# Weights requested ahead of batch 1's rows, O of group 0 directly behind its H, and batch 1 on the later batches' path, in a fused attention and MoE kernel

## Chip, cores and metric

One core of one Trainium2 chip. The metric is device time in microseconds (us) of one execution. Most executions of a kernel here agree within 1 to 2%. A few executions are in a slower state (those over 1.5% above the fastest of their kernel count as slow): every ratio uses fast runs alone, the medians are over all runs, and every profiled run was a fast one. Times inside an execution are counted from the start of the profiled span, which is some 2 us shorter than the device time.

## The reference, cut to what matters

```python
# q, k, v: (8 batches, 8 heads, 576 positions, 64), f32
rel    = pos[:, None] - pos[None, :]
scores = q @ k.T / 8 - slope[h] * abs(rel)
scores = where((rel >= 0) & (rel < 128), scores, -1e9)   # a causal window of 128
x      = softmax(scores) @ v                             # laid out as (4608 tokens, 512)
h      = x @ w_in                                        # w_in  512 x 2048
g      = h * sigmoid(beta * h)
out    = g @ w_out                                       # w_out 2048 x 512
```

The kernel works in bf16. It makes the columns of x batch by batch (attention) and eats them in nine groups of 512 tokens: **H** of a group is 16 x 4 matmuls with W1 (w_in), **O** is 4 x 4 *quarters* of four matmuls each with W2 (w_out). A batch has 576 tokens, so group 0 needs only batch 0, group 1 needs batch 1 too.

## The kernel before: the parts that matter

Every q, k and v row block is requested by SyncE as f32, cast to bf16 by GpSimd and, from batch 2 on, transposed by a DMA that SyncE issues as well. Weights are requested by GpSimd and cast on the way.

```python
def get(what, b, sb):                 # 128 rows of one of q, k, v: SyncE
    f = fst_pool.tile([P, H, D], F32, ...)                       # 13 buffers
    return nc.sync.dma_start(out=f[0:rows], in_=src[b, :, ...].rearrange("h p d -> p h d"))

def cast_qk(b, sb):                   # GpSimd, 4 buffers
    ...
    nc.gpsimd.tensor_copy(out=t[0:rows, 0], in_=fs.pop(("q", b, sb))[0:rows])
    return nc.gpsimd.tensor_copy(out=t[0:rows, 1], in_=fs.pop(("k", b, sb))[0:rows])

def DT(b, sb):                        # the transpose by DMA: SyncE
    nc.sync.dma_start(out=QK[b % 2][...], in_=src[0:rows]..., transpose=True)

def load_w2(n):                       # a quarter of W2: GpSimd; load_w1 is alike
    return nc.gpsimd.dma_start(out=W2[:, bass.ts(n, 4), :], in_=W2v[:, bass.ts(n, 4), :])

def SC(b, m, p):                      # later path: scores of two heads into SS (one tile)
    ...  # TensorE matmuls from QK, exp on ScalarE into pt, mask on VectorE
```

Batches 0 and 1 have a path of their own ("pairs"): rows come as pairs of heads, TensorE transposes them (`TP`), the bias is added by a matmul with a table (`SP_`), and the last 64 rows of each of these batches are done separately (the *tail*: `TT`, `SCT`, `PV`, `X`). The order of the opening before:

```python
# batch 0's pairs ... first W1 requests in between ...
after(get_pair(1, 0), w1[1])           # batch 1's rows behind two quarters of W1
... # the other rows of batch 1, the tails of batches 0 and 1
cast_pair(1, 0); cast_pair(1, 1); cast_v(1, 0); cast_v(1, 1); cast_pair(1, 2)
w2 = [load_w2(0), load_w2(1)]          # W2 behind most casts of batch 1
cast_pair(1, 3)
w2 += [load_w2(2), load_w2(3)]
... # TensorE: H of group 0, batch 1's pairs and tail 0 between; then H of group 1 with
    # tail 1 and the 16 + 8 O quarters of groups 0 and 1 between; then groups 2 to 8
```

The softmax here doesn't subtract the row's maximum and nothing guards it: scores larger than these inputs give would overflow.

## Time and profile before

| | before |
|---|---|
| device time, median of 4 runs | 352.47 us (349.71 to 357.34) |
| profiled span, mean granted clock | 350.1 us, 0.989 |
| TensorE busy, matmuls | 324.5 us (93%), 2289 |
| SyncE's DMA queue | 145,312 packets, 38.30 MB |
| GpSimd's DMA queue | 6,944 packets, 13.11 MB |
| first H / H of group 1 / group 2 | 23.0 / 61.70 / 109.3 us |

Of these 4 runs the one of 357.34 us is slow by that rule. The other three have a median of 351.21 us, and the later jobs measured this kernel at 350.86 to 351.08.

The prediction shows the slices, the stretches and the timelines of TensorE and ScalarE. One view of the kernel before is to be added, since the argument turned on it: SyncE's requests (columns: start, us that the issue took, queue, line, operation, tile and source, how many). These are batch 1's rows, requested after most of W1 had come and before any of W2 was asked for:

```profile
27.47 2.57 SPq L242 DMA_DIRECT2D fst<-in_q_dram  x1
...
31.80 1.91 SPq L234 DMA_DIRECT2D fst<-in_k_dram  x2
33.80 0.46 SPq L242 DMA_DIRECT2D fst<-in_q_dram  x1
```

Most requests of this stretch take 0.5 to 1.3 us each to issue; with W2 in flight, from 43 us on, three of four take 3.3 to 6.2.

### The profile page before, as it was taken

How to read it: one execution, taken by the hardware profiler on the slowest of the kernel's cores; microseconds unless marked ns; L12 is line 12 of the kernel's file. 1: busy time of each engine (PE TensorE's matmuls, PEld its weight loads, DVE VectorE, ACT ScalarE, POOL GpSimd, SP SyncE). 2: the span in 40 equal slices, each digit the busy share in tenths (PEclk: the TensorE clock that was granted, in tenths of full speed). 3: DMA queues.
4: the chain of work that ended last, by engine and by line, in shares of the span. 5: the costliest groups of instructions: out<-in, count | busy, mean ns of one | idle time of the engine just before them, and what ended most of it. 6: DMA issues, size and time to landing. Idle time of an engine off the chain costs nothing.

```text
span 350.1 us, 6218 instructions
## 1 busy us (share of the span) xinstructions
PE 324.5 (93%) x2289; PEld 151.4 (43%) x2289; DVE 192.3 (55%) x422; ACT 206.9 (59%) x396; POOL 111.5 (32%) x208
## 2 busy tenths in 40 slices
PE   6886886998999999998999999999999999999995
PEld 2442443443444444443444444444444444544442
DVE  7445576454754776476627763674477455614500
ACT  2545663548856776566657775675687566426511
POOL 4793624633735333503131324242200100010010
PEclk9899999899999999999999999999999999999999
DMA  7998999999999999991286989799311201120012
GB/s 176 228 195 204 194 186 202 177 201 220 217 230 237 239 211 226 212 198 48 57 182 133 182 175 227 129 222 166 93 32 53 77 30 47 30 99 0 30 62 90
DMA packets 152285, 51.79 MB, mean 148 GB/s; under 512 B 143664, under 2 KB 149824, under 8 KB 152256
## 3 DMA queue, kind: packets, MB, share of 16 engines
q1 hardware_dynamic: 145312, 38.30, 57.5%
q0 software_dynamic: 6944, 13.11, 14.9%
q8 instruction: 18, 0.29, 0.4%
q14 instruction: 11, 0.09, 0.1%
HBM read 36.71 MB, written 9.44 MB: 132 GB/s over the span
## 4 chain that ended last, share of the span: by engine, by line
PE 67%; ACT 11%; DVE 10%; DMA 6%; issue 3%; SPq 3%; POOL 0%; POOLq 0%; ACTq 0%
PE ops L530 31%; PE hps L507 26%; ACT pt L434 8%; DVE gT L515 4%; DVE pt L438 4%; PE SS L424 3%; DMA W<-in_moe_w_in_dram 3%; ACT sig L514 2%; SPq L234 2%; DMA fst<-in_k_dram 2%; PE pv L463 2%; PE pv L459 1%; DMA fst<-in_q_dram 1%; DVE xn L349 1%; PE SS L324 1%
## 5 line engine op out<-in xcount | busy, mean ns | idle before, releaser
L507 PE MATMUL hps<-XT,W 128*128 128x512 bf16 x560 | 141.5, 382 | 5.6 <-DVE gT L515 4.0
L530 PE MATMUL ops<-W,gT 128*128 128x512 bf16 x576 | 139.0, 379 | 0.0
L515 DVE SCALAR_TENSOR_TENSOR gT<-sig,hps 128x512 bf16<-128x512 bf16 x140 | 94.7, 683 | 76.4 <-ACT sig L514 75.7
L514 ACT ACTIVATE sig<-hps,beta_h 128x512 bf16<-128x512 f32 x140 | 95.8, 694 | 61.4 <-PE hps L507 56.1
L434 ACT ACTIVATE pt<-SS,bias 128x256 bf16<-128x256 f32 (+1 forms) x192 | 75.0, 478 | 11.4 <-PE SS L424 11.3
L507 PEld LDWEIGHTS <-W 128*128 128x128 bf16 x576 | 51.5, 98 | 62.6 <-issue 11.8
L530 PEld LDWEIGHTS <-gT 128*128 128x128 bf16 x576 | 52.4, 98 | 58.1 <-issue 2.1
L543 POOL DMA_DIRECT2D out_dram<-osb x34 | 18.4, 542 | 136.2 <-ACT osb L536 134.4
L438 DVE TENSOR_TENSOR pt<-pt,mask 128x1024 bf16<-128x1024 bf16 x48 | 38.0, 792 | 26.7 <-ACT pt L434 26.7
L536 ACT ACTIVATE osb<-ops 128x512 f32<-128x512 f32 x36 | 21.6, 600 | 44.6 <-PE ops L530 44.6
L265 POOL CAST vs<-fst 128x512 bf16<-128x512 f32 (+1 forms) x40 | 25.0, 636 | 37.4 <-DMA fst<-in_v_dram 32.5
L252 POOL CAST bst<-fst 128x512 bf16<-128x512 f32 (+1 forms) x32 | 20.7, 647 | 32.5 <-DMA fst<-in_q_dram 22.9
L349 DVE TENSOR_TENSOR xn<-pv,zs 128x256 bf16<-128x256 f32 (+1 forms) x64 | 26.9, 421 | 1.7
L348 DVE RECIPROCAL zs<-pv 128x4 f32<-128x4 f32 (+1 forms) x80 | 14.0, 176 | 22.3 <-PE pv L463 13.3
L253 POOL CAST bst<-fst 128x512 bf16<-128x512 f32 (+1 forms) x32 | 21.0, 656 | 10.2 <-DMA fst<-in_k_dram 10.0
L463 PE MATMUL pv<-vs,pt 128*128 128x65 bf16 x240 | 21.4, 193 | 0.0
L424 PE MATMUL SS<-qkT 64*128 64x256 bf16 (+2 forms) x240 | 18.9, 252 | 2.6 <-ACT pt L434 2.4
L463 PEld LDWEIGHTS <-pt 128*128 128x128 bf16 x240 | 16.5, 97 | 8.4
L341 ACT ACTIVATE pt<-SS 128x768 bf16<-128x768 f32 (+1 forms) x12 | 10.6, 881 | 15.5 <-PE SS L335 15.4
L424 PEld LDWEIGHTS <-qkT 64*128 64x128 bf16 x240 | 8.4, 94 | 23.1 <-issue 22.7
L459 PE MATMUL pv<-vs,pt 128*128 128x65 bf16 x192 | 17.9, 193 | 0.0
L459 PEld LDWEIGHTS <-pt 128*128 128x128 bf16 x192 | 15.2, 98 | 5.6
(78 smaller groups left out, 148.5 us busy)
## 6 DMA issues: line engine op xcount, KB each, us to landing
out_dram<-osb POOLq DMA_DIRECT2D x34, 256.0 KB, 3.3
fst<-in_q_dram SPq DMA_DIRECT2D x32, 256.0 KB, 4.8
fst<-in_v_dram SPq DMA_DIRECT2D x32, 256.0 KB, 4.0
fst<-in_k_dram SPq DMA_DIRECT2D x24, 256.0 KB, 5.2
fst<-in_k_dram SPq DMA_DIRECT2D x24, 128.0 KB, 4.0
W<-in_moe_w_in_dram POOLq DMA_DIRECT2D x4, 512.0 KB, 9.5
W<-in_moe_w_out_dram POOLq DMA_DIRECT2D x4, 512.0 KB, 11.1
fst<-in_q_dram SPq DMA_DIRECT2D x8, 128.0 KB, 3.3
```

The source lines that it names most:

```text
L265: return nc.gpsimd.tensor_copy(out=VS[b % 2][0:rows, sb, :, 0:D], in_=fs.pop(("v", b, sb))[0:rows])
L349: nc.vector.tensor_tensor(out=xn, in0=pv[0:nq, :, 0:D], in1=zs[0:nq].broadcast_to([nq, 4, D]), op=ALU.mult)
L424: nc.tensor.matmul(o, lhsT=qk[64 * e : 64 * e + 64, 1, p, P * kb : P * kb + P], rhs=qk[64 * e : 64 * e + 64, 0, p, P * kb : P * kb + nq], ...
L434: nc.scalar.activation(out=pt[:, e, cols], in_=sps[:, e, cols], func=ACTF.Exp, scale=qscale, bias=bias[:, half, h : h + 1],)
L438: nc.vector.tensor_tensor(out=pt[:], in0=pt[:], in1=masks[m][:], op=ALU.mult)
L459: nc.tensor.matmul(pv[:, hl, 0 : D + 1], lhsT=weights(b, qb - 1, h, 1), rhs=vs[:, qb - 1, h, 0 : D + 1], start=True, stop=False,)
L463: nc.tensor.matmul(pv[:, hl, 0 : D + 1], lhsT=weights(b, qb, h, 0), rhs=vs[:, qb, h, 0 : D + 1], start=qb == 0, stop=True,)
L507: nc.tensor.matmul(hps[:], lhsT=W1[:, c, bass.ts(j, P)], rhs=XT[:, c, c0 : c0 + TOKG], start=(c == 0), stop=(c == NDM - 1),)
L514: nc.scalar.activation(out=sig[:], in_=hps[:], func=ACTF.Tanh, scale=beta_h[:, j : j + 1])
L515: nc.vector.scalar_tensor_tensor(out=gts[g][:, j, :], in0=sig[:], scalar=1.0, in1=hps[:], op0=ALU.add, op1=ALU.mult)
L530: nc.tensor.matmul(ops_, lhsT=gT[:, j, i * P : i * P + P], rhs=W2[:, j, :], start=(j == 0), stop=(j == NFF - 1),)
L536: nc.scalar.mul(osb[:], ops_, 0.5)
```

## The change

Its intent: let TensorE go from H of group 0 straight to its O, by asking for all weights at once; drop batch 1's pair path, which costs TensorE transposes, table matmuls and permuting matmuls; and start batch 0 a little sooner by borrowing PSUM banks. The diff, cut to its core:

```diff
+    def room(b, wide, shape, name):          # new: batch 0 may use H's PSUM banks
+        if b == 0 and wide:
+            return psum_h.tile(shape, F32, name=name + "h", tag="hps")
+        return psum_t.tile(shape, F32, name=name, tag="t")
 ...
-    for b in range(2, B):                    # the later path
+    for b in range(1, B):
 ...
+            cast_pair(0, 3)
             w1.append(load_w1(0))
-            cast_pair(0, 3)
-            w1.append(load_w1(1))
+            cast_v(0, 2)
+            cast_v(0, 3)
+            w1 += [load_w1(n) for n in range(1, 4)]
+            betas()
 ...
-            betas()
+            w2 = [load_w2(0)]
             constants_late()
+            w2 += [load_w2(n) for n in range(1, 4)]
+            constants_masks()
 ...
-        after(get_pair(1, 0), w1[1])         # and all of the pair path of batch 1
+        b1 = blocks(1, [tail])               # rows, casts, DMA transposes of batch 1
+        b1.insert(6, tail_casts)             # casts of batch 0's tail: behind block 0's
+        gate = True
+        for job in b1:
+            r = job()
+            if gate:
+                after(r[0], w1[0])
+                gate = False
 ...
+        att[4:4] = tails                     # batch 0's tail behind four score groups
 ...
+        items = HG(0)[3:] + two(0) + OG(0, 2) + OG(0, 3)
+        spread(items, len(items) - 5, len(items) - 1, NP)
```

More of the change, by code (lines that the diff above doesn't have):

```diff
@@ L130, in constants @@
         make_identity(nc, ident[:])
+        make_identity(nc, identf[:])
         nc.gpsimd.iota(
@@ L188, in betas @@
         bps = psum_t.tile([P, NFF], F32, name="bps", tag="t")
-        make_identity(nc, identf[:])
         nc.tensor.transpose(out=bps[:], in_=bflat[:], identity=identf[:])
@@ L216 @@
     staged = {}
+    moved = set()
     def get(what, b, sb):
@@ L263, in cast_v @@
     def cast_v(b, sb):
+        moved.add(("v", b, sb))
         rows = ROWS[sb]
@@ L342, in SP_ @@
         pts[b, vis, p] = pt
+    WIDE = (("B", 0), ("B", 1))
+    def room(b, wide, shape, name):
+        if b == 0 and wide:
+            return psum_h.tile(shape, F32, name=name + "h", tag="hps")
+        return psum_t.tile(shape, F32, name=name, tag="t")
     PLACES = {0: ((0, 0),), 1: ((0, 128), (1, 256)), 2: ((1, 128), (2, 0)), 3: ((2, 384), (3, 256))}
@@ L357, in PVP @@
         pt = pts.pop((b, vis, p))
-        pv = psum_t.tile([P, 4, 66], F32, name="pv", tag="t")
+        pv = room(b, (vis, p) in WIDE, [P, 4, 66], "pv")
         q0 = 0 if vis == "A" else 2
@@ L372, in XP @@
         xn = xns.pop((b, "p", p))
-        xt = psum_t.tile([P, 4, P], F32, name="xtp", tag="t")
+        xt = room(b, p < 2, [P, 4, P], "xtp")
         for n in range(4):
@@ L402, in DT @@
         src = staged.pop((b, sb))
+        moved.add((b, sb))
         nc.sync.dma_start(
@@ L411, in SC @@
     def SC(b, m, p):
+        assert all((b, sb) in moved for sb in range((3, 5)[m]))
         qk = QK[b % 2]
@@ L442, in weights @@
         p, e = divmod(h, 2)
-        if b < 2:
+        if b < 1:
             at = 512 * e + 64 * p + (256 if kb == 3 else 0)
@@ L449, in PV @@
     def PV(b, qb, g):
+        assert ("v", b, qb) in moved
         nq = ROWS[qb]
@@ L587 @@
             before = pvx(b, ((0, 1), (2, 3, 4))[m])
-        if b + 1 < B:
+        if b == 1:
+            here += before
+            before = []
+        if 2 < b + 1 < B:
             js, all_, n = jobs(b + 1), here, len(here)
@@ L601, in place_of @@
         b, s = divmod(tok - 1, S)
-        return place[b, s // P] if b >= 2 else 0
+        return place[b, s // P] if b else 0
     need = [place_of(TOKG * (g + 1)) for g in range(NTG)]
@@ L639 @@
             PVP(0, "A", 2)
+            PVP(0, "B", 0)
             SP_(0, "B", 3)
-            cast_v(0, 2)
-            cast_v(0, 3)
-            w1 += [load_w1(n) for n in range(2, 4)]
-            PVP(0, "B", 0)
             PVP(0, "B", 1)
+            PVP(0, "A", 3)
             idle(1)
+            PVP(0, "B", 2)
             XP(0, 0)
-            PVP(0, "B", 2)
             idle(1)
             XP(0, 1)
-            PVP(0, "A", 3)
+            PVP(0, "B", 3)
             idle(1)
             XP(0, 2)
-            PVP(0, "B", 3)
-            idle(1)
-            betas()
+            w2 = [load_w2(0)]
             constants_late()
+            w2 += [load_w2(n) for n in range(1, 4)]
+            constants_masks()
             opening.close()
@@ L665 @@
                 Hm(0, j, range(3, 4))
-        def tail(b):
-            return [lambda: TT(b), lambda: SCT(b), lambda: PV(b, 4, 0), lambda: PV(b, 4, 1),
-                    lambda: X(b, 4)]
-        after(get_pair(1, 0), w1[1])
-        for n in range(1, NP):
-            get_pair(1, n)
-            if n == 1:
-                get("v", 1, 0)
-                get("v", 1, 1)
-        get("v", 1, 2)
-        get("v", 1, 3)
-        for b in range(2):
-            for w in "qkv":
-                get(w, b, 4)
@@ L683 @@
-        cast_pair(1, 0)
-        cast_pair(1, 1)
-        cast_v(1, 0)
-        cast_v(1, 1)
-        cast_pair(1, 2)
-        w2 = [load_w2(0), load_w2(1)]
-        cast_pair(1, 3)
-        w2 += [load_w2(2), load_w2(3)]
-        cast_v(1, 2)
-        cast_v(1, 3)
-        for b in range(2):
-            cast_qk(b, 4)
-            cast_v(b, 4)
-        constants_masks()
-        second = [
-            lambda: TP(1, 0), lambda: SP_(1, "A", 0), lambda: (TP(1, 1), SP_(1, "B", 0)),
-            lambda: SP_(1, "A", 1), lambda: PVP(1, "A", 0), lambda: (TP(1, 2), SP_(1, "B", 1)),
-            lambda: PVP(1, "A", 1), lambda: SP_(1, "A", 2), lambda: (TP(1, 3), SP_(1, "B", 2)),
-            lambda: PVP(1, "B", 0), lambda: (SP_(1, "A", 3), PVP(1, "A", 2)),
-            lambda: (XP(1, 0), PVP(1, "B", 1)), lambda: SP_(1, "B", 3),
-            lambda: (XP(1, 1), PVP(1, "B", 2)), lambda: PVP(1, "A", 3), lambda: XP(1, 2),
-            lambda: PVP(1, "B", 3), lambda: XP(1, 3),
-        ] + tail(0)
@@ L706, with blocks @@
-        done = 0
-        for j in range(3, NFF):
-            HS(0, j)
-            to = len(second) * max(0, j + 1 - 5) // (NFF - 5)
-            while done < to:
-                second[done]()
-                done += 1
-        work = tail(1)
-        b2 = jobs(2)
-        after_w2 = [True]
-        for n in range(5):
-            s, j = b2.pop(0)
-            r = j()
-            if after_w2[0]:
-                after_w2[0] = False
-                after(r[0], w2[1])
+        def blocks(b, between):
+            r = []
+            for sb in range(NQB):
+                r.append(lambda sb=sb: (get("q", b, sb), get("k", b, sb)))
+                if sb >= 2:
+                    r.append(lambda sb=sb: (cast_qk(b, sb - 2), DT(b, sb - 2)))
+                if sb == 2:
+                    r += between
+            for i in (0, 1):
+                r.append(lambda i=i: (cast_qk(b, 3 + i), DT(b, 3 + i)))
+                r.append(lambda i=i: get("v", b, i))
+            for sb in range(NQB):
+                if sb + 2 < NQB:
+                    r.append(lambda sb=sb: get("v", b, sb + 2))
+                r.append(lambda sb=sb: cast_v(b, sb))
+            return r
@@ new lines, in tail, with tail_casts @@
+        def tail():
+            for w in "qkv":
+                get(w, 0, 4)
+        def tail_casts():
+            cast_qk(0, 4)
+            cast_v(0, 4)
+        b1 = blocks(1, [tail])
[6 more added lines that the diff above has]
+                gate = False
+        tails = [(None, f, w) for f, w in (
+            (lambda: TT(0), 1), (lambda: SCT(0), 3), (lambda: PV(0, 4, 0), 2),
+            (lambda: PV(0, 4, 1), 2), (lambda: X(0, 4), 2))]
@@ L724 @@
+        att[4:4] = tails
+        for key in place:
+            place[key] += len(tails)
+        need[:] = [n + len(tails) for n in need]
         OG = lambda g, i: [lambda n=n: OS(g, i, n) for n in range(4)]
         HG = lambda g: [lambda j=j: HS(g, j) for j in range(NFF)]
-        h = HG(1)
-        items = h[:4]
-        o = OG(0, 0) + OG(0, 1) + OG(0, 2) + OG(0, 3) + OG(1, 0) + OG(1, 1)
-        for n in range(12):
-            items += [h[4 + n]] + o[n : n + 1]
-        items += o[12:]
@@ L732 @@
-        done, dw, dj = 0, 0, 0
+        two = lambda g: [f for p in zip(OG(g, 0), OG(g, 1)) for f in p]
+        done = 0
         def spread(items, first, last, target):
@@ L746, in spread, with wrap @@
                     done += 1
-        def wrap(it, n):
+        items = HG(0)[3:] + two(0) + OG(0, 2) + OG(0, 3)
+        spread(items, len(items) - 5, len(items) - 1, NP)
+        b2, dj = blocks(2, []), 0
+        def wrap(it, n, of):
             def f():
-                nonlocal dw, dj
-                it()
-                while dw < min(len(work), len(work) * (n + 1) // 10):
-                    work[dw]()
-                    dw += 1
-                while dj < min(len(b2), len(b2) * (n + 1) // 24):
-                    b2[dj][1]()
-                    dj += 1
-            return f
-        spread([wrap(it, n) for n, it in enumerate(items)], 17, len(items) - 2, need[2])
+                nonlocal dj
+                while dj < min(len(b2), of(n)):
+                    b2[dj]()
+                    dj += 1
+                it()
+            return f
+        spread([wrap(lambda: None, n, lambda n: 12 * (n + 1) // 10) for n in range(10)], 0, 10, need[1])
+        h, o = HG(1), two(1)
+        items = h[:6]
+        for n in range(2):
+            items += [h[6 + 2 * n], o[2 * n], h[7 + 2 * n], o[2 * n + 1]]
+        items += [h[10], h[11], h[12], o[4], h[13], o[5], h[14], h[15], o[6], o[7]]
+        spread([wrap(it, n, lambda n: 13 + n) for n, it in enumerate(items)], 2, len(items) - 1, need[2])
         for g in range(2, NTG):
```

## The prediction

> **What bounds the kernel now.** I read the page's forty slices first, to see where TensorE is not full:
>
> ```profile
> PE   6886886998999999998999999999999999999995
> PEclk9899999899999999999999999999999999999999
> DMA  7998999999999999991286989799311201120012
> ```
>
> One slice is 8.75 us. Holes in TensorE lie in the first seven slices (to about 61 us), while the DMA row stands at 8 or 9 tenths. From slice 20 on DMA is idle much of the time and TensorE is full. So an opening limited by data and latency goes before a TensorE-bound body. The chain of waits agrees: 67% PE, and in the opening one long transfer that the first batch-1 request is gated on:
>
> ```profile
> 15.38 9.27 DMA W<-in_moe_w_in_dram
> ```
>
> Second, the instruction order of both programs. From the first H of group 2 to the end the 1528 matmuls are the same in both, in the same order. In the timeline before, that H starts at 109.3 us, so the remaining 240.8 us should stay, and **the whole question is when group 2 starts**. Third, the stretches around that point (columns: length, busy us of PE, PEld, DVE, ACT and POOL, granted clock, DMA share, GB/s):
>
> ```profile
> 61.70:80.95 19.25, 19.25 (x118) 8.52 (x117) 8.41 (x16) 9.10 (x13) 9.02 (x22) 0.91 0.96 194
> 80.95:109.30 28.35, 25.92 (x206) 12.09 (x206) 17.14 (x35) 20.26 (x50) 13.66 (x21) 1.00 1.10 215
> 109.30:180.00 70.70, 68.43 (x477) 31.73 (x475) 42.57 (x85) 46.61 (x98) 23.67 (x42) 1.00 0.92 183
> ```
>
> Only 2.4 us of TensorE idle lie in 80.95 to 109.3. Fourth, the TensorE timeline, for how fast scores (SS) can follow each other, and ScalarE's for the same time:
>
> ```profile
> 81.04 0.39 PE L424 MATMUL SS<-qkT 64*128 64x256 bf16 x4
> 81.37 1.04 PE L507 MATMUL hps<-XT,W 128*128 128x512 bf16 x4
> 83.09 0.39 PE L424 MATMUL SS<-qkT 64*128 64x256 bf16 x4 [0.69 <-ACT pt L434]
> ```
>
> ```profile
> 81.48 1.57 ACT L434 ACTIVATE pt<-SS,bias 128x256 bf16<-128x256 f32 x4 [0.51 <-PE SS L424]
> 82.92 0.70 ACT L514 ACTIVATE sig<-hps,beta_h 128x512 bf16<-128x512 f32 x1
> 83.53 1.57 ACT L434 ACTIVATE pt<-SS,bias 128x256 bf16<-128x256 f32 x4
> ```
>
> SS exists once. A score group starts at 81.04, ScalarE reads it from 81.48 to 83.05, the next starts at 83.09: a **period of 2.05 us**, in which TensorE has 0.33 us of its own work; one H or O quarter (four matmuls, 0.864 us start to start) beside it still leaves 0.7 to 1.05 us idle. The last view is the tail of batch 0:
>
> ```profile
> 58.88 0.20 PE L459 MATMUL pv<-vs,pc 128*128 128x65 bf16 x1 [0.15 <-ACT pc L394]
> 60.55 0.23 PE L482 MATMUL xt<-ident,xn 64*128 64x64 bf16 x2 [1.02 <-DVE xn L349]
> 61.09 0.23 PE L482 MATMUL xt<-ident,xn 64*128 64x64 bf16 x2 [0.31 <-DVE xn L349]
> 61.70 2.95 PE L507 MATMUL hps<-XT,W 128*128 128x512 bf16 x8 [0.38 <-DVE XT L488]
> ```
>
> From the first PV to the last transpose 2.4 us pass for 0.8 us of work. The eight matmuls after it took 2.95 us instead of 1.73, at a granted clock of 0.91 over that stretch.
>
> **What the Trainium skill says.** "TensorE: Matmul & The Clock Gate", What's actually happening: the clock halves after an idle window of about 3.4 us and comes back after as long a busy one. The trace has it: mean clock 0.74 in 60 to 65 us, after the tail above. "DMA: Bandwidth & Descriptors", Issuing engines are not separate DMA queues: requests from SyncE and GpSimd share 16 engines and interleave. The trace agrees: the four W2 requests, issued at 39.6 to 43.0 us beside rows, took 7.4, 10.1, 12.1 and 14.4 us to land (the four W1 requests 9.2 to 11.9). "Perfetto Trace Analysis", Optimizing Tensor Performance (Matmuls), says that independent groups should rotate through PSUM banks so that evacuation overlaps; here an H run has two banks, and H start to gT end is 2.31 us (45.30 to 47.61), so two H take 2.31 us instead of 1.73.
>
> **The change part by part.** I walk the new order with these durations.
>
> 1. *Batch 0, and the first H.* The last cast goes ahead of the W1 request, which moves from 12.9 to about 15.0 us. By then most rows of batch 0 have landed, so W1's first quarter lands about 21 to 22 us (22.1 before). More PSUM slots, one filler matmul less and the early identity take about 0.8 us off. First H: 23.0 becomes **22.2 us**.
> 2. *H of group 0, uninterrupted.* First three with their wait: 3.7 us as before. Of the other 13, seven have free banks (7 x 0.864 = 6.0) and six go at the two-bank rate (3 x 2.31 = 6.9): 13.0 us, 1.8 of it bubble. End: **39 us**. W1 before landed at 22.1, 24.7, 27.2 and 30.1 us, a quarter each 2.5 to 2.9 us. With all four requests about as early, the last lands near 31, and is needed at 35: no wait.
> 3. *O of group 0.* 16 quarters = 13.8 us. W2's first request goes out near 20 us, the other three behind the late constants (7.6 us of GpSimd) near 28 to 30.5. Before, W2's end at 57.4 us had all batch-1 rows, two tails and some of batch 2 ahead of it; with about 2.9 MB fewer, at some 205 GB/s, that is 14 us earlier: 43. It is needed at 44.2. Twelve quarters end at 49.4 us.
> 4. *Scores of batch 1.* Three blocks must have gone through cast and DMA transpose. GpSimd casts block 0 after the masks (35 us), then waits for the tail rows of batch 0 (requested near 37, landing near 43), and only then casts blocks 1 and 2; the third transpose is issued near 47, 4.1 us to landing: **52 us**, a wait of 2 to 3 us. Four score groups with one O quarter each: 3 x 2.05 to the last start, 2.0 to its end: 60.2.
> 5. *Batch 0's tail, and the second half of batch 1, with no H or O beside them.* SS again, 0.95 us of matmuls, 1.03 us of exp and the latencies: 62.3. PV and transpose, 2.0 us (a little under the 2.4 above, as no gT stands between): 64.3. Four score groups: 8.2 us, then mask 0.7 and latency: 73.4. The five PV halves left are bound by VectorE (0.18 + 0.42 us each, with two copies of 0.42) and two psum_t buffers: some 4.7 us. H of group 1 starts at **78.1 us**. From 60.2 on that is 18 us for about 6.5 us of matmuls.
> 6. *H of group 1 with batch 2's attention and two O.* 24 quarters (20.7), attention 6.7, the next batch's first two score groups and a transpose 0.9: 28.3 us of TensorE. ScalarE: 16 sig of 0.62, 10 score groups of 1.57, 2 evictions of 0.6 = 26.8 us, and its score groups can begin only after four H. Latency on top, 4 us: 32.3. End: 110.4.
> 7. *Clock.* In step 5 TensorE is busy about a third of the time; I add 2 us for a halved clock there and in the first H behind it. **Group 2 starts near 112.4 us.**
>
> What is saved: batch 1's transposes on TensorE, bias-table matmuls, permuting matmuls and tail. The pair path costs about 10.4 us of TensorE (32 transposes at 0.057, eight score groups at 0.75, 56 PV at 0.031, 16 permutes at 0.057) and its tail 2.0; the later path 6.8: **5.6 us less**. What is given: bubbles in steps 2, 4, 5 and 6. Before, 17 us of bubble lay between 23.0 and 109.3 us; in the new order I count some 25 between 22.2 and 112.4. Sum: 112.4 - 109.3 = +3.1 us, span 353.2. As the gains and losses nearly cancel and each bubble is rounded upwards, I take +1.3 us on the median of 353.7: **355.0 us**.
>
> **The rivals.** *A: DMA was the bound of the opening, and weights first pays in full.* For it: DMA 8 to 9 tenths through 61 us, and O of group 0 beginning only at 68.9 us for want of W2 and places. If the data lets the scores of batch 1 start at 49.4, the clock stays up and step 6 costs its 28.3 us, group 2 starts at 104 and the time is about 346 to 348. Against it: the gain is handed to a latency-bound stretch. *B: the stretch without H and O is worse.* The cast of batch 1's last block needs the staging buffer which batch 0's tail frees only at its transposes (about 59 us), and the transposes and v rows stand behind it in SyncE's queue. If these land near 65 to 69 and TensorE runs at half clock throughout, 5 to 8 us more: 360 to 363. For it: tail rows that took 8 to 16 us to land at 40 to 46 us before. Against it: that was beside W2, now mostly done by then. *C: the order of DMA is hidden anyway*, and only the 5.6 us of matmuls count: 348. Against it: TensorE is not full there.
>
> **Range and chances.** Runs before span 349.7 to 357.3, so the median alone wanders 1%. Rival A's end is 346, B's 363; eight in ten between **347 and 362**. Faster by over 2% (below 346.6) needs all of A: 0.13. Slower by over 2% (above 360.8) needs B: 0.17. Within 2%: 0.70.
>
> **What would show it.** Step 1 to 3: first H near 22, H of group 0 back to back to 39, first O near 39, W2 not waited for over 1.5 us. Step 4: first batch-1 score near 52, held by a transfer into qkT. Step 5: H of group 1 near 78, TensorE busy a third between 60 and 78, a granted clock below 1. Step 6: group 2 near 112, ScalarE about 85% busy there. Wrong if the span after group 2's start is not near 241 us, if group 2 starts before 106 (the bubbles were oversized), or if H waits for W1.

## The result

| | before | changed |
|---|---|---|
| device time, median of 4 runs | 352.47 us | 363.82 us (363.8 to 365.31) |
| ratio, 95% interval | | 1.036 (1.0279 to 1.044): slower |
| profiled span, clock | 350.1 us, 0.989 | 361.7 us, 0.956 |
| TensorE busy, matmuls | 324.5 us, 2289 | 320.9 us, 2176 |
| SyncE's DMA queue | 145,312 packets, 38.30 MB | 153,088 packets, 39.48 MB |
| first H / H of group 1 / group 2 | 23.0 / 61.70 / 109.3 us | 21.97 / 86.32 / 120.6 us |

A ratio is the mean time of one kernel's fast runs over the mean of the other's fast runs of the same rounds, so not quite the ratio of the two medians. Some matmul records are missing in the changed kernel's trace: it has 2,214 weight loads for its 2,176 matmuls.

From group 2 on nothing changed: 241.1 us against 240.8. The whole loss lies before it. The forty slices of the changed kernel (9.04 us each):

```profile
PE   7688954658799899999899999999999999999995
PEclk9999995855999999999999999999999999999999
DMA  8899989999999999697173997699502111120012
```

Against the rows of before, the first five slices are a little fuller in sum (38 tenths against 36), and a new hole stands in the sixth to eleventh (45 to 99 us), in three of which the clock also falls to 0.5. DMA stays at 8 or 9 tenths throughout the hole. The stretches (columns as in the prediction) put numbers on it:

```profile
39.99:50.51 10.52, 10.47 (x48) 4.67 (x48) 1.37 (x2) 1.91 (x4) 0.72 (x3) 1.00 1.09 204
50.51:67.65 17.14, 7.67 (x40) 2.55 (x41) 2.39 (x4) 6.93 (x18) 8.74 (x15) 0.70 0.97 185
67.65:86.32 18.67, 11.55 (x151) 8.40 (x151) 12.14 (x35) 7.74 (x18) 8.64 (x15) 0.57 1.13 231
```

Twelve of the 16 quarters of O of group 0 run without a gap at full clock from 39.99 to 50.51. Then nothing is ready. TensorE's timeline says for what (in brackets: idle before, and what ended it):

```profile
39.99 10.52 PE L543 MATMUL ops<-W,gT 128*128 128x512 bf16 x47
56.11 0.40 PE L436 MATMUL SS<-qkT 64*128 64x256 bf16 x2 [5.59 <-DMA qkT<-bst]
59.12 0.39 PE L436 MATMUL SS<-qkT 64*128 64x256 bf16 x2 [2.62 <-DMA qkT<-bst]
...
86.32 0.58 PE L520 MATMUL hps<-XT,W 128*128 128x512 bf16 x1 [0.52 <-DVE XT L501]
```

Two scores of batch 1 wait for the DMA transpose of their q and k, the second until 59.12. The chain of waits, cut to that stretch, follows it back (start, us, what):

```profile
14.89 5.56 DMA W<-in_moe_w_in_dram
...
20.95 18.38 DMA fst<-in_k_dram
...
39.39 0.62 POOL bst L254
...
48.37 3.88 DMA fst<-in_q_dram
...
55.70 3.38 DMA qkT<-bst
```

The k rows of batch 1's first block took **18.38 us** from request to landing. Those of 48.37, which are of the same size but went out when the weights had come, took 3.88. SyncE's queue, to be held against the lines of before:

```profile
20.95 0.74 SPq L225 DMA_DIRECT2D fst<-in_k_dram  x1
21.78 5.97 SPq L225 DMA_DIRECT2D fst<-in_q_dram  x1
27.85 6.42 SPq L225 DMA_DIRECT2D fst<-in_k_dram  x1
34.36 6.03 SPq L225 DMA_DIRECT2D fst<-in_q_dram  x1
40.48 3.44 SPq L225 DMA_DIRECT2D fst<-in_k_dram  x1
...
46.26 0.73 SPq L225 DMA_DIRECT2D fst<-in_q_dram  x1
```

Three requests of 256 KB fill 21.78 to 40.39 us, worked out 42 GB/s. What was moved meanwhile, 3.54 MB in 21.97 to 39.99 us, divides between GpSimd's queue (q0) and SyncE's (q1) like this (packets, MB, share of the 16 engines' time):

```profile
q0 software_dynamic: 2921, 2.90, 95.2%
q1 hardware_dynamic: 2465, 0.62, 26.1%
```

The weights (requested by GpSimd between 14.9 and 30 us) take four fifths of the bytes, the rows under one. After 46 us a request takes 0.6 to 0.7 us again, and 0.6 to 1.4 in 54 to 86 us. Full DMA engines alone don't make the difference: their share is 1.22 in 21.97 to 39.99 us and still 1.13 in 67.65 to 86.32. GpSimd, which casts in order, waits with the rows:

```profile
39.39 0.61 POOL L254 CAST bst<-fst 128x512 bf16<-128x512 f32 x1 [5.15 <-DMA fst<-in_k_dram]
49.59 0.61 POOL L253 CAST bst<-fst 64x512 bf16<-64x512 f32 x1 [9.59 <-DMA fst<-in_q_dram]
```

The 9.59 us are for batch 0's tail rows; blocks 1 and 2 of batch 1 are cast only behind these, from 51.80.

"Perfetto Trace Analysis", DMA Instruction — HWDGE (DVE, Sync), of the Trainium skill, says how to read SyncE's lines: the reported window runs from the end of the semaphore wait until the descriptors are generated, and the movement of data is not in it. The trace agrees: the request at 48.37 has a window of 0.63 us, and its rows land after 3.88 us. So I read windows of 6 us not as the transfer itself but as requests that SyncE cannot hand over; whatever the reason, everything queued behind them waits.

### The profile page after: what moved, and what is told of

Same layout as the page of the kernel before. It is cut to its first block, busy times and chain, and to the rows that moved or that the text cites. A ratio compares the mean times of both kernels' runs of the same rounds, so it can differ in the third digit from the quotient of the medians.

```text
span 361.7 us, 6046 instructions
## 1 busy us (share of the span) xinstructions
PE 320.9 (89%) x2176; PEld 151.1 (42%) x2214; DVE 193.0 (53%) x421; ACT 211.0 (58%) x419; POOL 111.4 (31%) x208
## 3 DMA queue, kind: packets, MB, share of 16 engines
q1 hardware_dynamic: 153088, 39.48, 58.9%
## 4 chain that ended last, share of the span: by engine, by line
PE 59%; ACT 12%; DMA 10%; DVE 9%; SPq 5%; issue 3%; POOL 1%; POOLq 0%; ACTq 0%
PE ops L543 27%; PE hps L520 24%; ACT pt L446 9%; DMA fst<-in_k_dram 5%; DVE pt L450 4%; PE SS L436 4%; DVE gT L528 3%; SPq L225 2%; DMA fst<-in_q_dram 2%; ACT sig L527 2%; PE pv L476 2%; DMA W<-in_moe_w_in_dram 2%; SPq L235 2%; PE pv L472 1%; DVE xn L359 1%
## 5 line engine op out<-in xcount | busy, mean ns | idle before, releaser
L543 PE MATMUL ops<-W,gT 128*128 128x512 bf16 x558 | 136.6, 382 | 2.4 <-DVE gT L528 1.4
L446 ACT ACTIVATE pt<-SS,bias 128x256 bf16<-128x256 f32 (+1 forms) x224 | 87.7, 478 | 22.3 <-PE SS L436 22.3
L543 PEld LDWEIGHTS <-gT 128*128 128x128 bf16 x576 | 52.9, 98 | 61.8 <-issue 3.6
L450 DVE TENSOR_TENSOR pt<-pt,mask 128x1024 bf16<-128x1024 bf16 x56 | 42.7, 762 | 49.8 <-ACT pt L446 49.7
L436 PE MATMUL SS<-qkT 64*128 64x256 bf16 (+2 forms) x280 | 23.6, 263 | 14.5 <-DMA qkT<-bst 8.2
L253 POOL CAST bst<-fst 128x512 bf16<-128x512 f32 (+1 forms) x36 | 23.1, 641 | 40.5 <-DMA fst<-in_q_dram 37.9
L359 DVE TENSOR_TENSOR xn<-pv,zs 128x256 bf16<-128x256 f32 (+1 forms) x72 | 30.0, 420 | 1.8
L254 POOL CAST bst<-fst 128x512 bf16<-128x512 f32 (+1 forms) x36 | 22.7, 631 | 18.8 <-DMA fst<-in_k_dram 18.7
L476 PE MATMUL pv<-vs,pt 128*128 128x65 bf16 x280 | 26.5, 201 | 1.0 <-DVE pt L450 1.0
L436 PEld LDWEIGHTS <-qkT 64*128 64x128 bf16 x280 | 10.8, 97 | 37.9 <-issue 36.3
L476 PEld LDWEIGHTS <-pt 128*128 128x128 bf16 x280 | 20.4, 102 | 9.8 <-DVE pt L450 1.2
L472 PE MATMUL pv<-vs,pt 128*128 128x65 bf16 x224 | 22.3, 200 | 0.6 <-DVE xn L359 0.5
L472 PEld LDWEIGHTS <-pt 128*128 128x128 bf16 x224 | 18.7, 102 | 6.9 <-DVE xn L359 0.9
L343 ACT ACTIVATE pt<-SS 128x768 bf16<-128x768 f32 x4 | 3.2, 811 | 10.2 <-PE SS L337 10.2
```

The costliest lines, as they stand in the source:

```text
L359: nc.vector.tensor_tensor(out=xn, in0=pv[0:nq, :, 0:D], in1=zs[0:nq].broadcast_to([nq, 4, D]), op=ALU.mult)
L436: nc.tensor.matmul(o, lhsT=qk[64 * e : 64 * e + 64, 1, p, P * kb : P * kb + P], rhs=qk[64 * e : 64 * e + 64, 0, p, P * kb : P * kb + nq], ...
L446: nc.scalar.activation(out=pt[:, e, cols], in_=sps[:, e, cols], func=ACTF.Exp, scale=qscale, bias=bias[:, half, h : h + 1],)
L450: nc.vector.tensor_tensor(out=pt[:], in0=pt[:], in1=masks[m][:], op=ALU.mult)
L472: nc.tensor.matmul(pv[:, hl, 0 : D + 1], lhsT=weights(b, qb - 1, h, 1), rhs=vs[:, qb - 1, h, 0 : D + 1], start=True, stop=False,)
L476: nc.tensor.matmul(pv[:, hl, 0 : D + 1], lhsT=weights(b, qb, h, 0), rhs=vs[:, qb, h, 0 : D + 1], start=qb == 0, stop=True,)
```

## The experiments

Fifteen kernels ran. Unless said otherwise, times are medians, and the ratio is against the kernel before in the same rounds. The first four started from the theory that step 4's wait for batch 1's q and k was the whole loss, with rivals: the weights' place in the queue, the halved clock, and the order of GpSimd's casts.

**1. Tail casts later.** The 9.59 us wait taken out from before blocks 1 and 2:

```diff
-        b1.insert(6, tail_casts)
+        b1.insert(9, tail_casts)
```

> The changed kernel with one move: the casts of batch 0's tail rows on GpSimd stand behind batch 1's block 2 instead of behind its block 0. In the changed kernel GpSimd waited 9.6 us for those tail rows (to 49.6 us) with blocks 1 and 2 standing behind them, and the third transpose landed at 59.1. Theory 1 (batch 1's rows are starved by the weights in flight: they themselves land only near 44 to 46 us): the third transpose lands near 52 to 53, about 6 us earlier, the first score group is no earlier than 50, the span falls by 5 to 7 us to 355 to 357. Theory 2 (order on GpSimd alone; the rows were there by 33 as predicted): blocks 1 and 2 are cast right after block 0 and the transposes land by 49; no wait at all, the span falls by 9 us or more.

Measured: 362.07 us, 1.0299 (1.0252 to 1.0345), less of a gain than either theory had forecast. Requests went no faster (6.20, 6.42, 5.97 us), block 2 was cast from 47.5 instead of 52.9. Its first H came late in the profiled run (25.6, see experiment 9), so the scores that waited did so at 55.26 and 57.70. From the first O to the end it took 316.3 us, in the changed kernel 321.7, but that is no gain by itself: a later first H shortens the wait for rows that come when they come. In the medians the gain is 1.8 us. The order of casts matters a little; it is not the main cause.

**2. W2 behind the cast of block 2.**

```diff
-            w2 = [load_w2(0)]
             constants_late()
-            w2 += [load_w2(n) for n in range(1, 4)]
 ...
         b1.insert(6, tail_casts)
+        b1.insert(10, lambda: [load_w2(n) for n in range(4)])
```

> The changed kernel with all four W2 requests moved behind the cast of batch 1's block 2. Theory 1 (W2 in flight starves the rows): SyncE's row requests no longer take 6 us each, the first k rows are cast before 35 us (39.4 in the changed kernel), the third transpose lands by 47 (59.1). W2 then lands near 50 to 60 and O of group 0 waits for it, so the whole is not expected to gain: span 358 to 366. Theory 3 (the rows are slow for a reason of their own, such as their 256-byte pieces): the first cast stays near 39 and the span grows by 8 us or more.

Measured: 371.62 us, 1.0572 (1.0519 to 1.0624), worse than the 358 to 366 forecast. The rows were no longer held up: with W1 alone in flight the issues took 5.38 and 3.41 us, and 0.6 to 1.1 us from 31 us on; the first k was cast at 32.37 instead of 39.39. But O now waited for its weights, and W2, requested at 43.48, held up two transposes that SyncE issued at 45.16:

```profile
51.31 0.58 PE L543 MATMUL ops<-W,gT 128*128 128x512 bf16 x1 [10.68 <-DMA W<-in_moe_w_out_dram]
```

```profile
45.16 12.41 SPq L414 DMA_TRANSPOSE qkT<-bst  x2
```

So the weights in flight are what slows SyncE's requests, and the loss can't be taken away by moving W2 back in this order of TensorE's work.

**3. No wait for q and k of batch 1.** Scores of batch 1 read a tile of zeros; all transfers stay. The result is wrong on purpose in batch 1's scores, though it still passed the tolerance.

```diff
+    QX = const.tile([P, 2, NP, NQB * P], BF16, name="qx")     # set to 0
 ...
-        qk = QK[b % 2]
+        qk = QX if b == 1 else QK[b % 2]
```

> Wrong result on purpose: batch 1's scores read a tile of zeros, so they wait for no row, cast or transpose; all transfers are still made, and every instruction on TensorE, ScalarE and VectorE is kept. It measures what waiting for batch 1's q and k costs in the changed kernel. My prediction's sum missed by 8.2 us and I put that to this wait: first score group right behind the twelfth O quarter at 50.4 us (59.1 for its second half before), no idle of over 1 us between 50 and 60, span 351 to 354 (gain 8 to 10). Rival (the stretch without H and O costs most, whatever the data): gain of 4 us or less.

Measured: 363.96 us, 1.0363 (1.0309 to 1.0416): **nothing gained**. The wait was gone (first score at 51.77) and H of group 1 began 7 us sooner, at 79.35. Yet group 2 began at 121.1. The gain was given back at batch 3's first score, which had not waited before:

```profile
109.73 0.40 PE L438 MATMUL SS<-qkT 64*128 64x256 bf16 x2 [3.74 <-DMA qkT<-bst]
```

With this the theory that one wait explains the loss fell. The new theory: the rows of batches 1 to 3 come in one stream (request by SyncE, cast by GpSimd, transpose by SyncE), the change makes this stream late, and TensorE cannot reach group 2 before batch 3's first transposes, whichever score does the waiting. In the changed kernel itself no score waits for a transpose between 59.12 us and group 2: its own late start and the stream are two limits that lie close together, and only taking away the first made the second visible.

**4. Clock kept up.** Filler matmuls (zeros into an H bank) in the waits and between the scores of 50 to 86 us.

```diff
+    def warm_up(n):
+        t = psum_h.tile([P, TOKG], F32, name="fill", tag="hps")
+        for _ in range(n):
+            nc.tensor.matmul(t[:], lhsT=zeros[:, 0:P], rhs=zeros[:], start=True, stop=True, ...)
```

> The changed kernel with filler matmuls on zeros (into H's free banks) in the waits between 50 and 86 us: 36 while the first scores wait, 3 or 4 in each later wait of about 1 us, single ones at the end of batch 1. They only keep TensorE's clock up. The changed kernel ran at half clock from about 53 to 62 and 70 to 91 us. Theory A (latency-bound, so the halved clock costs only the start of H of group 1): granted clock near 1 between 53 and 91, gain 1.5 to 2.5 us. Theory B (the halved clock stretches every step of that stretch): gain 4 to 6 us. If the clock does not stay up, it says nothing.

Measured: 362.43 us, 1.0308 (1.0254 to 1.0363), clock 0.995. With the clock at full speed through the whole hole (1.00 in 50 to 86 us, 0.64 in the changed kernel), 1.4 us of the median came back. The halved clock is a consequence, not the cause.

**5. No wait for q and k of batches 1 to 3.** As 3, for three batches:

```diff
-        qk = QK[b % 2]
+        qk = QX if 1 <= b <= 3 else QK[b % 2]
```

> Wrong result on purpose: the scores of batches 1, 2 and 3 read zeros and wait for none of their own q and k; all transfers, casts and transposes are still made. In the run with this for batch 1 alone H of group 1 began 7 us earlier (79.4 against 86.3) but group 2 did not (121.1 against 120.6): a score group of batch 3 waited 3.7 us for its transposed block and the clock fell once more. Theory 'stream' (the rows of batches 1 to 3 come through one stream of requests, casts and transposes, which is late as a whole): with none of them waited for, group 2 starts near 113 and the span is 353 to 356. Rival 'schedule' (TensorE's own order loses the time again elsewhere): the span stays within 2 us of the changed kernel's 361.7.

Measured: 354.91 us, 1.0111 (1.0033 to 1.0188); group 2 near 113.9 in the profile. Where zeros for batch 1 gave nothing, zeros for batches 1 to 3 gave 8.9 us. That is the theory of the stream: one wait removed moves to the next link, all removed and the loss is gone but for 1.1%.

**6. Batch 1's DMA transposes left out** (on top of 3; rows and casts kept):

```diff
         moved.add((b, sb))
+        if b == 1:
+            return
```

> Wrong result on purpose: as the run with zeros for batch 1's scores, and batch 1's five DMA transposes are left out; its rows are still requested and cast. It prices the transposes that batch 1 has only since the change. If the stream is full and the five transposes take their share of it (from 44 to 63 us SyncE's queue had 5 transposes of 1.2 to 2.2 us and waits for casts): batch 2's last transpose is issued 5 us or more earlier than 84.6, batch 3's than 110.3, span 355 to 358. If they fit in idle time of the DMA engines: span 361 to 364 as with zeros alone.

**7. Its q and k rows and casts left out too.**

```diff
+            if b == 1:
+                r.append(lambda: (get("v", 1, 0), get("v", 1, 1)))
+                ...                            # v rows only, tail casts first
+                return r
```

> Wrong result on purpose: as the last, and batch 1's q and k rows are not requested or cast at all (2.4 MB less). An upper limit of what batch 1's data costs the opening. Theory 'stream': batch 2 and 3 move up by 10 us or more, no wait for a transpose before 120, group 2 near 113, span 352 to 355. Rival 'schedule': 360 or more.

Measured: 356.19 us, 1.0139 (1.0081 to 1.0196), and 354.65 us, 1.0107 (1.0039 to 1.0175). The stream can be read off the issue of batch 3's last transpose. Before, in the changed kernel, and in experiment 7:

```profile
101.57 1.29 SPq L403 DMA_TRANSPOSE qkT<-bst  x1
```

```profile
110.29 1.22 SPq L414 DMA_TRANSPOSE qkT<-bst  x1
```

```profile
97.53 1.22 SPq L416 DMA_TRANSPOSE qkT<-bst  x1
```

It came 8.7 us later with the change, as group 2 did by 11.3; without the five transposes of batch 1 it came at 102.50, without its rows at 97.53. Against experiment 3 the five transposes are worth 7.8 us of the median. The rows are worth another 1.5, which isn't resolved, as the two intervals overlap. In 6 and 7 no score waits for q and k between 50 and 130 us.

**8. The kernel before, with W2 early and nothing else changed:**

```diff
             w1 += [load_w1(n) for n in range(2, 4)]
+            w2 = [load_w2(n) for n in range(4)]
 ...
         cast_pair(1, 2)
-        w2 = [load_w2(0), load_w2(1)]
         cast_pair(1, 3)
-        w2 += [load_w2(2), load_w2(3)]
```

> The kernel before with one part of the change: the four W2 requests directly behind the four W1 requests (near 20 us in place of 39.6 to 43). Theory 'starved rows' (requests of SyncE wait about 6 us each while weights are in flight): the first batch-1 rows, which landed at 30.9, land near 40, batch 1's attention slips, H of group 1 begins 4 to 8 us later than 61.7, span 354 to 358. Rival (weights first is harmless, as rows and weights are equal in sum): span within 2 us of 350.

Measured: 362.16 us, **1.0317** (1.027 to 1.0363). This one move gives nearly the whole loss, more than was forecast, on a kernel whose batch 1 doesn't use DMA transposes. SyncE's queue, and TensorE waiting for the casts of the same rows:

```profile
27.77 3.52 SPq L242 DMA_DIRECT2D fst<-in_q_dram  x1
31.38 7.48 SPq L224 DMA_DIRECT2D fst<-in_v_dram  x2
38.95 3.90 SPq L234 DMA_DIRECT2D fst<-in_k_dram  x2
```

```profile
34.46 0.61 PE L288 MATMUL tps<-ident,bst 128*128 128x128 bf16 x4 [4.96 <-POOL bst L258]
...
42.69 1.18 PE L288 MATMUL tps<-ident,bst 128*128 128x128 bf16 x8 [2.19 <-POOL bst L258]
```

The second pair of batch 1 was cast at 42.0 instead of 32.7, and H of group 1 began at 72.56 instead of 61.70. From there to the end it took 287.0 us, in the kernel before 288.4, and no score waited for q and k between 50 and 130 us: here the loss is batch 1's own rows, and the later batches add none.

**9. Beta's transpose back in its old place.** In the changed kernel TensorE waits 1.13 us at 16.34 for beta, which the change had moved up. Derived kernels reached their first H between 21.4 and 25.6 us.

```diff
             w1 += [load_w1(n) for n in range(1, 4)]
-            betas()
 ...
             XP(0, 2)
+            betas()
```

> The changed kernel with betas() back behind the last early transpose. In the changed kernel that small transpose, moved up, stands in TensorE's order before batch 0's fourth transposes and waited for beta's transfer (1.1 us at 16.3; 1.6 to 2.0 us in the runs derived from it, where the clock then fell and the first H came at 23.2 to 25.5 instead of 21.9). If that is a cost of its own: no such wait, first H at 21 to 22 in every run, gain 1 to 3 us, span 359 to 361. If the first H is held by W1 anyway: no gain.

Measured: 364.32 us, 1.0372 (1.0339 to 1.0405). A miss: that wait was gone and the first H came at 21.44, but the scores still began at 56.09 and 59.28, after waits of 6.50 and 2.80. Time saved ahead of a late stream is waited out.

**10 to 12. Parts of the change on the kernel before.** 10: batch 0 in H's PSUM banks, with the opening's order and the early identity. 11: three O quarters of group 0 put around batch 0's tail, into the hole that the prediction shows near 60 us. 12: both.

```diff
+        make_identity(nc, identf[:])                    # 10, 12: early
 ...
-        pv = psum_t.tile([P, 4, 66], F32, name="pv", tag="t")
+        pv = room(b, (vis, p) in WIDE, [P, 4, 66], "pv")  # 10, 12; XP alike
 ...
-        ] + tail(0)                                     # 11, 12
+        ] + tail(0)[:4] + [
+            lambda: (OS(0, 0, 0), OS(0, 0, 1), X(0, 4), OS(0, 0, 2)),
+        ]
```

> The kernel before with one part of the change: batch 0's products and transposes in H's PSUM banks, its order in TensorE's opening, one filler less and the early identity (beta's transpose stays late, the requests stay as before). By my step 1: first H at 22.2 instead of 23.0, but batch 1's rows are still gated on W1's second quarter near 24.7, so at most 0.8 us in all: ratio 0.997 to 1.000. If PSUM banks held the opening more than I thought: 1 to 2 us.

> The kernel before with three quarters of O of group 0 put into the hole around batch 0's tail (59.4 to 61.7 us), W2's first three quarters having landed at 47.0 to 54.4 us: the idea of the change (O right behind its H) where the data allows it. The hole of 2.2 us closes, and the clock does not halve behind it (that cost 1.7 us): gain 2.5 to 4 us, ratio 0.989 to 0.993. If what follows is bound by batch 2's and 3's rows as in the changed kernel, TensorE waits there instead and the gain is under 1 us.

> Both of the last two edits on the kernel before. If they add: ratio 0.987 to 0.992, span 346 to 347.5.

Measured, in 14, 22 and 22 runs: 351.11 us, 0.9997 (0.9968 to 1.0025); 350.70 us, 0.9994 (0.9971 to 1.0018); 351.87 us, 0.9992 (0.9966 to 1.0019). All the same as before (351.08 us in 51 runs of that job). The first H came at 21.53 in 10, and the hole was closed in 11, whose profiled run started group 2 at 105.96; the medians show none of it, so 11 and 12 are misses. 11's profile flatters it: of the 3.3 us by which its group 2 came sooner than in the profile before, 2.4 were there at the first PV of the tail, ahead of the edit (56.48 against 58.88), and its profiled run (349.10 us) was one of its fastest. These two parts of the change are worth nothing measurable without its order of DMA. Batch 1 on the later batches' path, the third part, was not tried alone.

**13. Experiment 5 with fillers**, those of experiment 4 behind the scores and PV of 50 to 86 us, without the ones that filled its waits:

```diff
-        qk = QK[b % 2]
+        qk = QX if 1 <= b <= 3 else QK[b % 2]
 ...
         att[4:4] = tails
+        more = {4: (0, 1), 5: (0, 4), 7: (0, 3)}   # fillers ahead of and behind a step
+        ...
```

> Wrong result on purpose: zeros for the scores of batches 1 to 3 (no wait for their q and k) and the filler matmuls in batch 1's bare stretch. With zeros alone the kernel was still 1.1% over the kernel before, at half clock from 60 to 84 us. If the halved clock is what is left: clock 1 there, gain 2 to 4 us, ratio 1.000 to 1.005. If it is the bare stretch itself (score groups every 2.05 us with nothing beside them): gain under 1.5 us, ratio 1.006 to 1.012.

Measured in 20 runs: 352.46 us, 1.004 (1.0012 to 1.0069), clock 0.993, group 2 at 110.63. The profile moved by 3.3 us against experiment 5 (113.93), but of the 1.1% that experiment 5 left no share is shown to be the halved clock's: its interval (1.0033 to 1.0188) contains 1.004. What is left here, 0.4%, is the schedule together with the derived kernel's later first H (23.54 instead of 21.97).

**14. O of group 0 spread among batch 1's scores**, with W2 behind the cast of block 2 and the tail casts behind that. If the order of TensorE's work were what made W2 urgent, this should have won.

```diff
-        b1.insert(6, tail_casts)
+        b1.insert(9, lambda: [load_w2(n) for n in range(4)])
+        b1.insert(10, tail_casts)
 ...
-        spread(items, len(items) - 5, len(items) - 1, NP)
+        spread([wrap(it, n, ...) for n, it in enumerate(items)], 12, len(items) - 1, need[1])
```

> The changed kernel with O of group 0 spread among batch 1's scores, batch 0's tail and batch 1's products (not directly behind H), all of W2 requested behind the cast of batch 1's block 2, and the tail rows' casts behind that. Theory 'W2 starves the rows, and O before them leaves nothing beside the scores': rows land by 36, first score near 43, O quarters in all of its gaps, H of group 1 near 71 to 74 (86 in the changed kernel), full clock, and a gain of 8 us or more unless batch 3's rows then hold TensorE (five transposes more than before): span 350 to 354. If the order of W2 is not the cause: 358 or more.

Measured: 370.48 us, 1.0563 (1.0499 to 1.0627). A large miss, and one line shows where it starts. Blocks 0 to 2 were cast by 37.3 us, as wanted; W2 was requested at once, from 37.27, and the next transpose ran into it:

```profile
38.92 13.26 SPq L414 DMA_TRANSPOSE qkT<-bst  x1
```

```profile
57.45 0.40 PE L436 MATMUL SS<-qkT 64*128 64x256 bf16 x2 [17.64 <-DMA qkT<-bst]
```

A transpose that mostly takes 1.2 to 2.7 us to issue in these traces took 13.26 us with W2 in flight. In the three places tried, W2 starved rows (the changed kernel) or transposes (2 and 14).

**15. The kernel before plus five idle transposes:** batch 1's cast rows are also transposed into a tile that nobody reads, ahead of batch 2's rows.

```diff
+        for p in range(4):
+            nc.sync.dma_start(out=QX[:, :, :, P * p : P * p + P]...,
+                              in_=staged[1, "p", p][:]..., transpose=True)
```

(and one more behind the cast of its tail)

> The kernel before with five idle DMA transposes more, of batch 1's cast rows into a tile that nobody reads, in SyncE's queue before batch 2's rows: the transposes that the change adds, alone. Leaving them out of the changed kernel gained about 8 us. If the stream of rows bounds the kernel before too: batch 2's and 3's transposes come 4 to 8 us later, and the span grows by 3 to 8 us. If it has slack before the change: under 1.5 us.

Measured: 355.78 us, 1.0127 (1.0072 to 1.0182): a loss in the range forecast. SyncE spent 9.4 us on them, 8.16 on four and 1.20 on the fifth at 60.28. But the profile doesn't show the loss to be theirs:

```profile
46.78 0.25 PE L365 MATMUL pv<-vs,pt 128*128 128x65 bf16 x3 [3.12 <-POOL vs L266]
51.15 8.16 SPq L695 DMA_TRANSPOSE qx<-bst  x4
```

TensorE lost 3.12 us to batch 1's last v rows, which landed late beside W2 (requested at 35.90 in this run, at 39.63 in the one before), and that was over before the first extra transpose was issued. H of group 1 began 3.03 us later (64.73), batch 3's last transpose slipped by 3.07 (101.57 to 104.64), and from H of group 1 to the end it took 288.3 us, before 288.4. The transposes did hold staging buffers (GpSimd waited 10.67 us for one, to 57.40), which might have cost time without the earlier wait. So whether the stream bounds the kernel before too is not shown; what five transposes cost is shown by 6 against 3 alone.

## Why the prediction was wrong

By its own steps, on the trace of the changed kernel:

- **Step 1, first H at 22.2: right** (21.97). **Step 2, H of group 0 until 39: right** (first O at 39.99, with waits of 0.63 to 0.64 us for gT every 2.52 us). **Step 3, twelve O quarters until 49.4, W2 not waited for: right** (50.51, no wait for W2 in the timeline).
- **Step 4, the first scores at 52 after a wait of 2 to 3 us: this is the step that failed.** They came at 56.11 and 59.12, after 5.59 and 2.62 us of idle. Two assumptions in it fell. The rows of block 0 were to be there when GpSimd had made the masks (35 us); the k rows landed at 39.3. The tail rows were to be requested near 37 and land near 43; they were requested at 46.26 and landed near 49.5. Both come of pricing SyncE's requests as if each had its turn beside the weights. Before, they had been seen at 0.5 to 1.3 us each, with few weights in flight; now three quarters of W1 and one of W2 were in flight when the first slow request was issued at 21.78, and three of them took 5.97 to 6.42 us each. The sign was in the trace before: three of the four requests issued at 43 to 57 us beside W2 took 3.3 to 6.2 us, and rival B named the late tail rows, but the step was not priced from them. Experiment 2, with W2 moved back, has no slow row request between 31 us, when W1 had come, and the request of W2 at 43.48, and experiment 8 shows W2's early place alone costing 3.2%.
- **Step 5, group 1 at 78.1: late by 8.2 us** (86.32), of which 7.1 stand already at the wait of step 4 (59.12 instead of 52). The clock was 0.57 there. **Step 6, 32.3 us and 2 for the clock: right** (34.28), but in part by luck: begun 7 us sooner, in experiment 3, the same step took 41.7 us (79.35 to 121.08), held by batch 3's transposes, which the step didn't have. The suffix of 240.8 was right (241.1).
- **The sum**: group 2 at 120.6 instead of 112.4 is 8.2 us too late, and the step that was put at 2 to 3 us is where it arose. The choice to put +1.3 on the median instead of the +3.1 worked out made the miss larger.
- **What the prediction did not have at all**: that later batches depend on the same stream. With 7 us of waiting taken out at batch 1 (experiment 3) the time stayed; only with batches 1 to 3 freed did it fall to 1.011. The five transposes that batch 1 adds to SyncE's queue were counted as a saving on TensorE (5.6 us less) and not as a cost elsewhere; they cost 7.8 us in the changed kernel (6 against 3). So had step 4 been right and its wait away, the stream would still have held group 2.
- **Of the rivals**, B was nearest: late data, a bare stretch, a halved clock, 360 to 363 us. It placed the lateness at the last block of batch 1 and a staging buffer, though, and the trace shows it at the first. A forecast 346 to 348 us if the data lets the scores start in time and the clock stays up. Experiment 13 granted both, and the changed order still stands at 1.004: A's gain isn't there. C, that the order of DMA is hidden anyway, fell with 8.
- **Readings of the trace before.** The two-bank rate was put at 2.31 us, from an H start at 45.30; the timeline has that start at 45.13, so 2.48, and the changed kernel ran at 2.52. The 17 us of bubble before are not idle time of the trace: there TensorE is idle for 11.9 of the 86.2 us, and in the changed kernel for some 24 of 98.6. That the clock halves is seen in the traces; the length of the idle window that the prediction cites is not. In the changed kernel the last matmul ahead of the wait ended at 50.51, and the mean clock was 1.00 in 51.5 to 52.5 us, 0.83 in 52.5 to 53.5 and 0.50 in 53.5 to 54.5: it fell some 2.6 us after that matmul (an estimate from these windows).

What stays open: how the 3.6% divide. W2 early alone gives 3.2% (8), on a kernel whose order of work is another one; leaving out batch 1's transposes gives back 2.2% (6 against 3). No run adds both to the kernel before, so whether they add up is not known, and in the changed kernel both later places tried for W2 (2 and 14) hurt more. And no run shows *why* SyncE's requests get so small a share. What the trace has is a difference of size: in 21.97 to 39.99 us SyncE's queue moves 0.62 MB in 2,465 packets, some 250 bytes each, GpSimd's 2.90 MB in 2,921, some 990 bytes each. "DMA: Bandwidth & Descriptors", Queues, rings and completion order, states that each DMA engine takes the queues in turns, and changes over after a whole packet; turns of equal number and unequal bytes would favour the weights. The nearly equal numbers and the rows' share of under a fifth fit that, if the trace's packets are those that the page means, but no experiment changed the packet sizes.

## What to carry to other kernels

Asking for everything early is not free when the queues share the engines: before a large transfer is moved forward, look at which small requests will be in flight with it, and price these by what such requests took *beside* such a transfer in the trace, not by what they took alone. Follow a late transfer to the last consumer of its stream; a wait that is removed at the first consumer may only move to the third, which a run that removes all of them tells apart at once. And count an operation moved from a busy engine to the DMA as a cost in the issuing queue: leaving out batch 1's five transposes gained 7.8 us here.

## What the Trainium skill lacked or had wrong

- "DMA: Bandwidth & Descriptors", Issuing engines are not separate DMA queues: it says that requests interleave, and that the time to initiate a DMA "is usually small relative to the DMA itself". The section doesn't say how unequal the shares can be, nor that initiating can become the long part: row requests of 256 KB took 5.97 to 6.42 us to issue beside the weights' requests and 0.6 to 0.7 us after them, with 0.62 of 3.54 MB moved.
- The same page, DMA Transpose (X-bar), gives no time for issuing one beside other traffic: mostly 1.2 to 2.7 us here, 13.26 us for one with W2 in flight.
- "Perfetto Trace Analysis", DMA Instruction — HWDGE (DVE, Sync): the window agrees (0.63 us reported, 3.88 us to landing), but it is not said that the window itself can grow tenfold beside another queue's requests (0.6 to 6.42 us), which is the sign by which this case could be read.
